# Rows of four tokens for q and k, whole rows for v and out, in a kernel of windowed attention and an MLP

## The chip, the cores and the metric

The kernel runs on one core of a Trainium2 chip. The metric is the device time of one execution in microseconds (us). TensorE is called PE here (PEld is its weight load), VectorE DVE, ScalarE ACT, GpSimd POOL and SyncE SP, as in the profile. Every engine works through its own queue of instructions in order. Transfers (DMAs) are issued by SP and ACT (the hardware queues, q1 and q10 in the profile) and by POOL (the software queue, q0).

## The reference

Attention over a window of 128 tokens and 4 sink tokens, for 4 batches of 8 heads, 768 tokens and 64 values per head, then an MLP with a sigmoid gate over the 3072 rows:

```
scores = q @ k.T / sqrt(64)                       # (4, 8, 768, 768)
keep   = (key < 4) | ((0 <= query - key) & (query - key < 128))
a      = softmax(where(keep, scores, -1e9))
x      = (a @ v), heads side by side              # (3072, 512)
h      = x @ w_in                                 # (3072, 2048)
out    = (h * sigmoid(1.702 h)) @ w_out           # (3072, 512), float32
```

All inputs are float32 in memory. The kernel works in fp16 and sums in float32.

## The kernel before

**Blocks.** The 3072 rows are cut into twelve blocks of 256 tokens (`TB`), three to a batch. For block k the kernel loads q, k and v, casts q and k to fp16, turns them on PE (transposes against `ident`, L447), copies the turned halves out of PSUM into `qkT` (L270), and multiplies keys by queries (L514, and L475 for the sink keys). ACT takes the exponential (L531, L483), DVE multiplies by the mask (L540, L544), PE multiplies by v (L574), DVE divides (L588, L590), PE turns the result (L597) and DVE or ACT copies it to `xT`. The MLP's first product (`mm1`, L631) makes 16 slabs of 128 columns for the block; ACT and DVE form the gate from them (L643, L645). The second product is `mm2`: for block 0 and the last block plainly (L781), for the others with seven products instead of eight of half size (L706), which needs sums of pieces of w_out made once by DVE (`sums`, L659).

**Tokens.** A partition holds two neighbouring tokens of each head, so that a run in memory is 2 x 64 float32 values, 512 bytes. A tile of 128 tokens therefore comes out of the transposes in two groups, the even and the odd tokens; v is loaded in the same order, by four transfers a block of 64 partitions each (L413), and the rows of `out` are written by two transfers of every second row for each 128 tokens (L756, L809). The mask and the places of the sink keys are made for that order. The last block goes back to natural order in its copies to `xT`.

**The plan.** The order of each engine's queue is worked out when the kernel is built. Every operation is given to `Plan` with the engines that may do it, an assumed duration, what it depends on and a due time (`prio`); `Plan.run` walks through time, gives each free engine the ready operation that is due first, and writes the instructions in that order. The chip does not know the plan's times. An instruction waits there only for what its data need (a tile that another engine writes or still reads) and, if it issues a DMA, for the one of eight places of its kind (eight for hardware queues, eight for the software queue) that it takes over from the DMA issued eight before it.

**Loads at the start.** `LOADS` puts the first transfers in order: a0 and v0 (block 0's q and k, and its v), a1, w0 (the first of four pieces of w_in), v1, w1, w2, w3, then the four pieces of w_out as w4, w6, w5, w7, then a2 and v2. q and k of block 0 come in eight transfers by head pairs, from SP and ACT (L369); those of later blocks in one transfer for q and one for k, from SP (L377). v and the weights are issued by POOL (L413, L333). `GATES` makes SP wait, before block 2's q, for w5 to land: SP issues a tiny transfer that reads it (L384). The casts of q and k are DVE's and ACT's for block 0, also POOL's for block 1, and POOL's alone from block 2 on.

**PE's order at the start** is attention of blocks 0 and 1 with `mm1` of block 0, then `mm1` of block 1 mixed with `mm2` of block 0 (64 and 32 matmuls, the latter of 512 columns), and only then the transposes of block 2, the first four matmuls into a bank from `qk16` of that block.

Of the kernel before, what the change touches and what calls it, by code (L numbers as in the profile page):

```python
# [15 lines left out]
D = 64  # L16
# [6 lines left out]
class Op:  # L23
    def __init__(self, engs, fn, deps, prio, acq, rel, kind):

        self.engs, self.fn = engs, fn
        self.deps = [d for d in dict.fromkeys(deps) if d is not None]
        self.prio, self.acq, self.rel, self.kind = prio, acq, rel, kind
        self.eng = self.start = self.end = self.banks = self.places = self.behind = None
        self.users = []  # L30

# [14 lines left out]
class Plan:  # L46
# [14 lines left out]
    def run(self, warm=None, warm_until=0.0, late_bank=0.0):  # L61
# [44 lines left out]
        while todo:  # L106
# [57 lines left out]
            for owner, i in o.rel:  # L164
                t = o.end + 80
                bank_free[owner.banks[i]] = t
                count[owner.acq[0]][owner.places[i]] = t
# [16 lines left out]
def kernel(  # L184
# [27 lines left out]
    SEVEN_FROM = 1  # L212
    NH = NF // 2
# [25 lines left out]
    qkT = ring("qkT", RKT, (P, 2, 2, NP, P), FP16)  # L239
# [17 lines left out]
    def f16(o, i=0):  # L257
        return bank[o.banks[i]][:, 0:256].bitcast(FP16)
# [30 lines left out]
    def make_mask():  # L289


        m = mask.rearrange("s (g u i a) -> s u g i a", g=2, u=2, i=2)
        nc.gpsimd.memset(mask, 1.0)
        for u, (keep, sign) in enumerate(((ALU.is_ge, 1), (ALU.is_gt, -1))):
            for h in range(2):
                a_ = m[64 * h : 64 * h + 64, u]
                nc.gpsimd.affine_select(out=a_, in_=a_, compare_op=keep, fill=0.0, base=-h * sign,
                                        pattern=[[0, 2], [sign, 2], [2 * sign, 64]], channel_multiplier=-2 * sign)
        for h in range(2):
            nc.gpsimd.memset(mask[64 * h : 64 * h + n_sink // 2, 0 : 2 * P], 1.0)  # L300

    o_ident = op("POOL", 350, 450, make_ident, prio=NEVER, kind="const")
    o_mask = op("POOL", 3000, 3100, make_mask, prio=NEVER + 1, kind="const")
# [37 lines left out]
    LOADS = ["a0", "v0", "a1", "w0", "v1", "w1", "w2", "w3", "w4", "w6", "w5", "w7", "a2", "v2"]  # L341

    GATES = {2: 5}
# [13 lines left out]
    def load(k):  # L357
# [4 lines left out]
        war = reuse("s32", sl)  # L362
        dst = qk32[sl].rearrange("p (e h i d) -> p e h i d", e=2, h=H, i=2)
        lq = {}
        if k == 0:
            for p in range(NP):
                for e, (eng, dma, src) in enumerate((("SP", nc.sync, q), ("ACT", nc.scalar, k_ap))):
                    def f(p=p, e=e, dma=dma, src=src):
                        dma.dma_start(  # L369
                            dst[:, e, 2 * p : 2 * p + 2],  # L370
                            src[b, 2 * p : 2 * p + 2, t0 : t0 + TB].rearrange("h (p i) d -> p h i d", i=2),
                        )
                    lq[p, e] = op(eng, 500, (450,), f, war, prio=NEVER + 2.5 + p / 8, kind="load")
        else:
            for e, src in enumerate((q, k_ap)):
                def f(e=e, src=src):
                    nc.sync.dma_start(  # L377
                        dst[:, e], src[b, :, t0 : t0 + TB].rearrange("h (p i) d -> p h i d", i=2)
                    )
                if k in GATES and e == 0:  # L380

                    j = GATES[k]
                    seen = w_in16[0:1, 0, 512 * j : 512 * j + 32] if j < 4 else w_out16[0:1, 4 * (j - 4), 0:32]
                    loads.append(op("SP", 100, (10,), lambda seen=seen: nc.sync.dma_start(gate, seen),  # L384
                                    [(o_win if j < 4 else o_wout)[2 * (j % 4)]], prio=prio - 0.1, kind="gate"))
                o = op("SP", 450, (1800,), f, war, prio=prio + 0.1 * e, kind="load")
                loads.append(o)
                for p in range(NP):
                    lq[p, e] = o

        c16 = qk16[k % RQ].rearrange("p (i e h d) -> p i e h d", i=2, e=2, h=H)
        war = reuse("qk16", k % RQ)
        w = 2 if k == 0 else 4
        for h0 in range(0, H, w):
            for e in range(2):
                def f(eng, h=slice(h0, h0 + w), e=e):
                    copy(eng, c16[:, :, e, h].rearrange("s i h d -> s h i d"), dst[:, e, h])

                ps = range(h0 // 2, (h0 + w) // 2)
                o = plan.any(cast(P * w, CAST_QK[k]), f, [lq[p, e] for p in ps] + war,  # L400
                             prio=nominal(k - 1, -7 + h0) if k else NEVER + h0, kind="cqk")
                for p in ps:
                    o_cqk[k, p, e] = o
        for o in {id(x): x for (kk, _, _), x in o_cqk.items() if kk == k}.values():
            uses("s32", sl, o)
        w16 = v16[k % RV]
        war = reuse("v16", k % RV)

        o_cv[k] = []
        for j in range(2):  # L410
            for i in range(2):
                src = v[b, :, t0 + P * j : t0 + P * j + P].rearrange("h (a i) d -> i a h d", i=2)[i]
                o = op("POOL", ISSUE, (600,), lambda i=i, j=j, src=src: nc.gpsimd.dma_start(  # L413
                    w16[64 * i : 64 * i + 64, j, :, 0:D], src), war + [o_ones],
                       prio=load_at(f"v{k}"), kind="load")
                loads.append(o)
                o_cv[k].append(o)
        if r == 0:

            def f():  # L420
                for t in range(2):
                    for i in range(2):
                        nc.gpsimd.tensor_copy(
                            out=vs16[64 * t + 32 * i : 64 * t + 32 * i + 2, b, :, i],
                            in_=w16[64 * t : 64 * t + 2, 0, i::2, 0:E],
                        )
            o_vs[b] = op("POOL", 1900, 2000, f, [*o_cv[k], o_vs0], prio=nominal(k - 1, 0), kind="vs")
# [4 lines left out]
    o_qkT, o_ks, o_se, o_m, o_xT = {}, {}, {}, {}, {}  # L432

    def front(k, p):
# [6 lines left out]
        c16 = qk16[k % RQ].rearrange("p (i e h d) -> p i e h d", i=2, e=2, h=H)  # L441

        def tp():
            ps = f16(o_tp).rearrange("d (e j i p) -> d e j i p", e=2, j=2, i=2)
            for i in range(2):
                for e in range(2):
                    nc.tensor.transpose(  # L447
                        ps[:, e, :, i, :], c16[:, i, e, 2 * p : 2 * p + 2].rearrange("s h d -> s (h d)"), ident
                    )

        if p == 0:
            o_T["war", k] = reuse("qkT", k % RKT)
        war = o_T["war", k]
        o_tp = op("PE", 4 * pe_ns(P), 3 * pe_ns(P) + P / 2.4 + 166, tp,
                  [o_cqk[k, p, 0], o_cqk[k, p, 1], o_ident] + war, prio=base - 5 * h8, acq=("t", 1), kind="tp")
        uses("qk16", k % RQ, o_tp)
# [426 lines left out]
```

## Time and profile before

| what | value |
|---|---|
| three runs | 230.84, 233.15, 233.51 us; median 233.15 |
| the profiled execution | 232.8 us, of which the core's span is 231.1 |
| busy in the span | PE 220.3 us, DVE 186.5, ACT 138.7, POOL 83.4 |
| mm1, L631 | 768 matmuls of 256 columns, 101.9 us |
| transposes of q and k, L447 | 192 matmuls, 18.8 us |
| copies of them to qkT, L270 | DVE 30 of 415 ns, ACT 18 of 586 ns |
| casts of q and k on POOL, L270 | 40 of 695 ns |
| issues of v on POOL, L413 | 48 of 698 ns |
| q and k of one block from SP | 2 x 512 KB; 7.4 and 8.4 us from issue to landing |
| out | 45 transfers of 128 KB; 2.6 us to landing |
| software queue | 29568 packets, 7.34 MB written, 33.2% of 16 engines' span |
| hardware queue of SP | 27808 packets, 18.22 MB, 30.5% |

A matmul's end is modelled in the profile, so a busy PE need not be at its peak; and sizes of packets are as written, so that a load that is cast from float32 to fp16 on its way counts half of what it reads. The mean granted clock was 0.993.

### The profile page before, as it was taken

How to read it: one execution, taken by the hardware profiler on the slowest of the kernel's cores; microseconds unless marked ns; L12 is line 12 of the kernel's file. 1: busy time of each engine (PE TensorE's matmuls, PEld its weight loads, DVE VectorE, ACT ScalarE, POOL GpSimd, SP SyncE). 2: the span in 40 equal slices, each digit the busy share in tenths (PEclk: the TensorE clock that was granted, in tenths of full speed). 3: DMA queues.
4: the chain of work that ended last, by engine and by line, in shares of the span. 5: the costliest groups of instructions: out<-in, count | busy, mean ns of one | idle time of the engine just before them, and what ended most of it. 6: DMA issues, size and time to landing. Idle time of an engine off the chain costs nothing.

```text
span 231.1 us, 6404 instructions
## 1 busy us (share of the span) xinstructions
PE 220.3 (95%) x2552; PEld 186.5 (81%) x2552; DVE 186.5 (81%) x424; ACT 138.7 (60%) x288; POOL 83.4 (36%) x157
## 2 busy tenths in 40 slices
PE   8869999899999999999999999999999999999994
PEld 7657786588888888988888988888988988898863
DVE  6657979889999979979979969979979869878520
ACT  3717653478688657657567657647657657634320
POOL 8769422399985342275524042233200000000000
PEclk9979999999999999999999999999999999999999
DMA  6999999999999655389215742064012012012042
GB/s 188 239 154 196 187 202 201 263 252 262 158 236 258 112 69 135 97 64 212 92 45 126 131 53 63 1 43 99 3 44 50 0 36 58 3 35 61 0 94 91
DMA packets 58639, 26.64 MB, mean 115 GB/s; under 512 B 26736, under 2 KB 55664, under 8 KB 58608
## 3 DMA queue, kind: packets, MB, share of 16 engines
q0 software_dynamic: 29568, 7.34, 33.2%
q1 hardware_dynamic: 27808, 18.22, 30.5%
q10 hardware_dynamic: 1232, 0.66, 1.0%
q8 instruction: 20, 0.33, 0.6%
q14 instruction: 11, 0.09, 0.1%
HBM read 27.26 MB, written 6.29 MB: 145 GB/s over the span
## 4 chain that ended last, share of the span: by engine, by line
PE 59%; DVE 16%; DMA 13%; POOL 5%; issue 3%; ACT 2%; SPq 0%; POOLq 0%; ACTq 0%; DVEq 0%
PE bank L631 24%; PE bank L706 21%; DMA w_out<-in_moe_w_out_dram 6%; DVE gT L645 4%; DMA v<-in_v_dram 4%; PE bank L574 3%; DMA qk<-in_q_dram 3%; PE bank L781 3%; DVE sm L676 3%; DVE at L540 3%; PE bank L447 3%; PE bank L514 2%; DVE xn L590 2%; PE bank L597 2%; ACT at L531 1%
## 5 line engine op out<-in xcount | busy, mean ns | idle before, releaser
L631 PE MATMUL bank<-xT,w_in 128*128 128x256 f16 x768 | 101.9, 273 | 0.2 <-DVE gT L645 0.2
L643 ACT ACTIVATE th<-bank 128x512 f16<-128x512 f32 x96 | 57.7, 601 | 48.1 <-PE bank L631 40.4
L631 PEld LDWEIGHTS <-w_in 128*128 128x128 f16 x768 | 71.9, 98 | 10.1 <-issue 1.8
L645 DVE SCALAR_TENSOR_TENSOR gT<-th,bank 128x512 f16<-128x512 f16 x96 | 64.9, 681 | 12.3 <-ACT th L643 11.7
L531 ACT ACTIVATE at<-bank 128x512 f16<-128x512 f32 (+1 forms) x96 | 49.4, 573 | 12.6 <-PE bank L514 11.5
L413 POOL DMA_DIRECT2D v<-in_v_dram x48 | 33.0, 698 | 24.7 <-PE bank L574 11.1
L270 POOL CAST qk<-qk 128x512 f16<-128x512 f32 x40 | 26.6, 695 | 33.0 <-PE bank L447 22.6
L706 PE MATMUL bank<-wt,sm 128*128 128x256 f16 x240 | 33.3, 273 | 0.6 <-DVE xT L270 0.6
L706 PEld LDWEIGHTS <-sm 128*128 128x128 f16 x320 | 29.9, 98 | 4.8 <-DVE sm L676 0.7
L540 DVE TENSOR_TENSOR at<-at,mask 128x1024 f16<-128x1024 f16 x32 | 22.5, 712 | 6.4 <-ACT at L531 6.3
L706 PEld LDWEIGHTS <-gT 128*128 128x128 f16 x240 | 22.5, 98 | 2.5
L574 PE MATMUL bank<-v,at 128*128 128x65 f16 x352 | 21.8, 195 | 2.7 <-DMA v<-in_v_dram 2.7
L706 PE MATMUL bank<-w_out,gT 128*128 128x256 f16 x160 | 21.4, 273 | 0.0
L731 DVE SCALAR_TENSOR_TENSOR osb<-bank,osb 128x256 f32<-128x256 f32 x50 | 20.5, 410 | 0.6 <-PE bank L706 0.6
L574 PEld LDWEIGHTS <-at 128*128 128x128 f16 x352 | 17.8, 99 | 3.7 <-DMA v<-in_v_dram 2.9
L590 DVE TENSOR_TENSOR xn<-bank,rcp 128x256 f16<-128x256 f32 x48 | 20.0, 417 | 0.5
L447 PE MATMUL bank<-ident,qk 128*128 128x128 f16 x192 | 18.8, 223 | 1.3 <-POOL qk L270 1.3
L483 ACT ACTIVATE ats<-bank 128x256 f16<-128x256 f32 x32 | 12.8, 401 | 9.0 <-PE bank L475 8.5
L447 PEld LDWEIGHTS <-qk 128*128 128x128 f16 x192 | 13.8, 100 | 2.8 <-POOL qk L270 1.5
L781 PE MATMUL bank<-w_out,gT 128*128 128x512 f16 (+1 forms) x80 | 15.0, 336 | 0.0
L597 PE MATMUL bank<-ident,xn 128*128 128x128 f16 x96 | 13.7, 226 | 1.3 <-DVE xn L590 1.2
L270 DVE COPY qkT<-bank 128x512 f16<-128x512 f16 x30 | 12.4, 415 | 3.2 <-PE bank L447 2.8
(48 smaller groups left out, 246.7 us busy)
## 6 DMA issues: line engine op xcount, KB each, us to landing
out_dram<-osb SPq DMA_DIRECT2D x45, 128.0 KB, 2.6
qk<-in_q_dram SPq DMA_DIRECT2D x11, 512.0 KB, 7.4
qk<-in_k_dram SPq DMA_DIRECT2D x11, 512.0 KB, 8.4
v<-in_v_dram POOLq DMA_DIRECT2D x48, 64.0 KB, 5.6
w_in<-in_moe_w_in_dram POOLq DMA_DIRECT2D x4, 512.0 KB, 8.5
w_out<-in_moe_w_out_dram POOLq DMA_DIRECT2D x4, 512.0 KB, 12.9
qk<-in_q_dram SPq DMA_DIRECT2D x4, 128.0 KB, 3.5
qk<-in_k_dram ACTq DMA_DIRECT2D x4, 128.0 KB, 3.7
```

The costliest lines, as they stand in the source:

```text
L270: {"POOL": nc.gpsimd.tensor_copy, "DVE": nc.vector.tensor_copy, "ACT": nc.scalar.copy}[e](out=out, in_=in_)
L413: o = op("POOL", ISSUE, (600,), lambda i=i, j=j, src=src: nc.gpsimd.dma_start(w16[64 * i : 64 * i + 64, j, :, 0:D], src), war + [o_ones], ...
L447: nc.tensor.transpose(ps[:, e, :, i, :], c16[:, i, e, 2 * p : 2 * p + 2].rearrange("s h d -> s (h d)"), ident)
L531: nc.scalar.activation(out=A[:, i, 0:W], in_=f32(o_s, 2 * n + i)[:, 0:W], func=AF.Exp, scale=scale)
L540: nc.vector.tensor_tensor(out=a_, in0=a_, in1=m_[:, 2 * P :].unsqueeze(1).to_broadcast((P, 4, 2 * P)), op=ALU.mult,)
L574: nc.tensor.matmul(avp()[:, j, i], a_, v_, start=(n == 0), stop=(n == len(mms) - 1))
L590: o_n = op("DVE", 333, 425, lambda: nc.vector.tensor_tensor(out=X[:, p].rearrange("s j (h d) -> s j h d", h=2), in0=avp()[:, :, :, 0:D], i ...
L631: nc.tensor.matmul(f32(holder[0])[:, bass.ts(e, TB)], w_in16[:, c, bass.ts(Fi, P)], X[:, c], start=(c == 0), stop=(c == NP - 1),)
L643: o_t = op("ACT", 477, 600, lambda first=first: nc.scalar.activation(out=th[first.places[0]], in_=f32(first), func=AF.Tanh, scale=0.851), ...
L645: o_g[k, s] = op("DVE", 595, 690, lambda first=first, s=s: nc.vector.scalar_tensor_tensor(out=g[:, 2 * s : 2 * s + 2].rearrange("p a t -> ...
L706: nc.tensor.matmul(f32(holder[bank_of])[:, 0:HM], x[:, Fi], w[:, Fi], start=first and Fi == 0, stop=Fi == NH - 1, skip_group_check=True)
L781: nc.tensor.matmul(f32(holder[0])[:, 0:w], g[:, Fi, bass.ts(j, P)], w_out16[:, Fi, c], start=(n + h == 0), stop=(n + h == NS),)
```

## The change

What it does, piece by piece:

- q and k are loaded with four tokens of a head in a partition (runs of 1 KB). A head's 256 tokens fill 64 partitions, so heads 0 to 3 lie in partitions 0 to 63 and heads 4 to 7 in 64 to 127, and each of q and k takes two transfers of 64 partitions (`g`) a block; for blocks 0 and 1 each is halved again by heads (`m`). A block from 2 on has four transfers of 256 KB where it had two of 512 KB.
- A new function `turn(k, m)` makes eight transposes into one whole bank of PSUM. Two copies take the bank out, one for each head pair, and put the tokens into natural order: they read with a step of 64 elements between neighbours. The bank is free when both are done (`readers = 2`).
- `qkT` is now (query or key, pair, token) in natural order; scores, sink keys, mask, v and out follow. v is two transfers of 128 partitions a block, out one transfer of 128 whole rows for each 128 tokens. Pairs are met in the order `HP = (0, 2, 1, 3)`, which the indices of v and w_in undo.
- Loads at the start: `o_go`, a memset of one element of block 1's q and k tile by POOL, is put after v0's issues, and SP's loads of block 1 wait for it; w0 is put after the sink keys of block 0's first two pairs; in `LOADS` a2 and v2 come before w_out; block 2's q and k wait for w2 and block 3's for w5.

The diff, cut to its core:

```diff
-    LOADS = ["a0", "v0", "a1", "w0", "v1", "w1", "w2", "w3", "w4", "w6", "w5", "w7", "a2", "v2"]
-    GATES = {2: 5}
+    LOADS = ["a0", "v0", "a1", "w0", "v1", "w1", "w2", "w3", "a2", "v2", "w4", "w6", "w5", "w7"]
+    GATES = {2: 2, 3: 5}
...
+    o_go = op("POOL", 80, 180, lambda: nc.gpsimd.memset(qk32[1][0:1, 0:1], 0.0), prio=NEVER + 14, kind="const")
...
-        war = reuse("s32", sl)
-        dst = qk32[sl].rearrange("p (e h i d) -> p e h i d", e=2, h=H, i=2)
+        war = reuse("s32", sl) + ([o_go] if k == 1 else [])
+        dst = qk32[sl].rearrange("p (e m x f) -> p e m x f", e=2, m=2, x=2)
...
+        n = 2 if k <= 1 else 1
+        for c in range(n):
+            ms = slice(c * 2 // n, (c + 1) * 2 // n)
+            for e, src in enumerate((q, k_ap)):
+                eng = "ACT" if (k, e) == (0, 1) else "SP"
+                for g in range(2):
+                    h0 = 4 * g + 2 * ms.start
+                    to = dst[64 * g : 64 * g + 64, e, ms].rearrange("p m x f -> p (m x) f")
+                    fr = src[b, h0 : h0 + 4 // n, t0 : t0 + TB].rearrange("h (a i) d -> a h (i d)", i=4)
+                    o = op(eng, 500, (730 / n,), lambda to=to, fr=fr, eng=eng: (
+                        nc.scalar if eng == "ACT" else nc.sync).dma_start(to, fr), war,
+                           prio=prio + 0.1 * (4 * c + 2 * e + g), kind="load")
...
-            for i in range(2):
-                src = v[b, :, t0 + P * j : t0 + P * j + P].rearrange("h (a i) d -> i a h d", i=2)[i]
-                o = op("POOL", ISSUE, (600,), lambda i=i, j=j, src=src: nc.gpsimd.dma_start(
-                    w16[64 * i : 64 * i + 64, j, :, 0:D], src), war + [o_ones],
+            src = v[b, :, t0 + P * j : t0 + P * j + P].rearrange("h s d -> s h d")
+            o = op("POOL", ISSUE, (1250,), lambda j=j, src=src: nc.gpsimd.dma_start(w16[:, j, :, 0:D], src),
...
+    def turn(k, m):
+        c16 = qk16[k % RQ].rearrange("p (m i e f) -> p m i e f", m=2, i=4, e=2)[:, m]
+        def tp():
+            ps = f16(o_tp).rearrange("d (g e i a) -> d e i g a", g=2, e=2, i=4)
+            for e in range(2):
+                for i in range(4):
+                    nc.tensor.transpose(ps[:, e, i], c16[:, i, e], ident)
...
+        o_tp.readers = 2
+        for g in range(2):
+            p = 2 * m + g
+            def cp(e, g=g, p=p):
+                copy(e, T[:, :, p].rearrange("d e (a i) -> d e a i", i=4),
+                     f16(o_tp)[:, 512 * g : 512 * g + 512].rearrange("d (e i a) -> d e a i", e=2, i=4))
+            o_qkT[k, p] = [plan.any(pick({"DVE": (600, 690), "ACT": (477, 600)}, COPY[k]), cp, [o_tp] + war,
+                                    prio=base + 2 * g * h8 - 5 * h8, rel=[(o_tp, 0)], kind="cp")]
...
-            for i in range(2):
-                def f(to=paired[i], fr=T[j][64 * i : 64 * i + 64], i=i):
-                    nc.sync.dma_start(to, fr)
-                o_d = op("SP", 500, (400.0,), f, after, prio=prio, kind="out")
+            o_d = op("SP", 500, (800.0,), lambda to=rows, fr=T[j]: nc.sync.dma_start(to, fr), after, prio=prio, kind="out")
...
+        for m_ in range(2):
+            turn(k_, m_)
...
+        if k_ == 0:
+            o_w[0].deps.append(o_ks[0, 1])
```

What the build makes of it, engine by engine: PE has the same matmuls apart from four more of its idle fillers. Of the 48 copies to `qkT` DVE does 22 and ACT 26 (before 30 and 18). The tile framework lets one engine at a time read a bank: in 18 of the 22 DVE copies the wait is for ACT's copy of the bank's other half, in the rest ACT waits for DVE or one engine does both. POOL issues 24 transfers of v, and after w3 its queue reads v2, w4, w6, w5, then the four casts of block 2, then w7 and v3; w4, w6 and w5 wait there only for the places that w0 and v1 held. PE's queue has, after attention of blocks 0 and 1, the 64 matmuls of `mm1` of block 0 and 24 of block 1's, and then the transposes of block 2; the other 40 of block 1's `mm1` and all of `mm2` of block 0 stand behind these.

## The prediction, made before the changed kernel was run

> **What bounds the kernel now.** I read the page first: PE is busy for 95% of the span, so time is won or lost where PE's order stops. The second view is the chain that ended last, in order of time, for the first 50 us (start, duration, what):
>
> ```profile
> 19.07 0.68 POOL w_in L333
> 19.75 1.45 POOL w_out L333 x2
> 21.20 13.77 DMA w_out<-in_moe_w_out_dram
> 34.99 0.63 SPq L384
> 35.66 7.13 DMA qk<-in_q_dram
> ...
> 45.54 0.87 POOL qk L270
> 46.45 0.56 PE bank L447 x7
> ```
>
> Block 2's q is issued at 35.66, when w5 has landed. It needs 7.13 us, k lands about 45.5, POOL casts it, and PE goes on with block 2's transposes at 46.45. Before that PE had run nearly without a hole from 27 us on and had finished `mm1` of blocks 0 and 1 and `mm2` of block 0. I call the 46.45 T, the time at which block 2's transposes can go on.
>
> Why did q take 7.13 us? The third view is the DMA queues, for the window from 35.7 to 38.0 us and then for 38 to 42 (queue: packets, MB, share of 16 engines):
>
> ```profile
> q0 software_dynamic: 2391, 0.33, 213.0%
> q1 hardware_dynamic: 40, 0.01, 2.5%
> ```
> ```profile
> q1 hardware_dynamic: 1892, 0.95, 92.1%
> q0 software_dynamic: 829, 0.10, 40.5%
> ```
>
> The hardware queue, though it had been given q, got almost nothing until about 38.0, when the software queue had finished what it was given earlier: w7, v2 and three of the four pieces of v3. The opposite case is from 6 to 9 us, where v0 had been issued from 4.50 on, but block 1's q and k at 3.50 and 3.92:
>
> ```profile
> q1 hardware_dynamic: 1739, 0.88, 109.2%
> ```
>
> No packet of v moved in that window. So both queues together are served about in the order of issue. This is the reading that my number hangs on.
>
> In the later blocks DVE is nearly full too. One block, in a window of 17 us (length, then busy PE, PEld, DVE, ACT, POOL):
>
> ```profile
> 94.00:111.00 17.00, 17.00 (x202) 14.86 (x200) 14.55 (x34) 11.52 (x25) 10.13 (x21) 1.00 0.83 122
> ```
>
> Over such windows from 77 to 213 us DVE is busy 14.3 to 15.2 of 17 us.
>
> **PE's order around block 2.** In the chain 48 matmuls of L781, 16384 columns, take 6.96 us, 0.109 us for 256 columns. The changed order leaves 40 matmuls of block 1's `mm1` (4.4 us) and `mm2` of block 0 (16384 columns, 7.0 us) behind block 2's transposes: 11.3 us of work that was ahead of them. If nothing else changed, the kernel would end at the same time for T = 46.45 - 11.3 = 35.1 us. Each microsecond of T above that is lost, and below it won, as far as PE arrives that early itself.
>
> **When PE arrives.** It needs w3 first. In the trace the weights land at about 2.54 us each (POOL's issues of v, let go by them, start at 27.63, 30.17, 32.71 and 35.26). w3 landed at about 27.5. The same bytes must come before w3 now; two things shorten it. The hole from 15 to 16 us (68 GB/s written there, 201 from 29 to 35) goes, 0.7 us: it came when POOL waited 2.77 us for a place held by v0, and with two issues of v a block that wait is gone. And 1-KB rows: the trace has no load with them; 512-byte rows moved at 294 GB/s (6 to 9 us), the weights' 2-KB rows at 1.05 MB in 2.54 us, 413 GB/s. I take 340, nearer to the 512-byte row, so that q and k of two blocks, 2.1 MB, take 6.2 us instead of 7.1: 0.9 us won (0 to 2.0). So w3 lands at 25.9, 16 matmuls end `mm1` of block 0 at 27.7, 24 more end at 30.3. v0 landed at 12.7; now it is issued 1.4 us earlier (three instructions of the mask fewer, 2 x 0.42 and 0.35, with hops) and without the 3 us of block 1's packets ahead of it. That moves attention of block 0 by some 4 us, but PE then waits for the weights, so the gain is contained in the 30.3.
>
> **When block 2 arrives.** SP now issues a2 when w2 has landed, 24.8 - 1.6 = 23.2 us. But POOL has by then issued v2, w4, w6 and w5: they wait only for places that w0 and v1 give back, and v1's last piece, issued at 12.97, had landed 4.8 us later, at 17.8, even before. By the order of issue a2 stands behind them. In the old run the software queue was through at 38.0; now w7 (2.54 us) and three quarters of v3 are no longer ahead (v moved 0.33 MB written, 0.66 read, in 2.3 us, so 0.39 MB takes 1.4), and 0.7 and 0.9 are saved as above: 38.0 - 2.5 - 1.4 - 0.7 - 0.9 = 32.5. From there to the landing of k it was 7.5 us with block 3's q behind it; at the least it is the transfer at the weights' rate, 2.5, plus 0.6. Block 3 now comes later, so I take 5.0, between the two. Then the cast and PE's start, 0.95 as before (45.5 to 46.45): T = 38.45. Bounds: 31.4 + 3.1 + 0.95 = 35.4 and 33.4 + 7.5 + 0.95 = 41.9. PE stands from 30.3 to 38.4, where it stood 1.5 us before. That is 3.35 us over break-even (0.3 to 6.8).
>
> The 11.3 us of matmuls now run beside more DVE work: the sums of w_out, 16 of 0.417 us, were done in the old stall's cover and stand now behind block 2's transposes. I take the pace of the later blocks for them: these come 17.28 us apart (an exponential on the chain starts at 84.70 and, two blocks on, at 119.26), and their matmuls at 0.109 us make 16.3. That is 6% of 11.3, 0.7 us (0 to 2).
>
> w7 is behind the casts of block 2 in POOL's queue: issued at about 41.5, landed at about 47. PE asks for it some 8 us of work after T, at 46.5. I take 0, at most 1.
>
> **The copies.** The last block of the old kernel already copies with a step of 64 elements into `xT`. DVE's copies in 201 to 207 us (stepped) and 160 to 196 (mostly plain; min/median/max):
>
> ```profile
> L270 DVE COPY xT<-bank x2: 424/424/424, 200.7 to 204.6; 128x256 f16<-128x256 f16 x2
> ```
> ```profile
> L270 DVE COPY xT<-bank x5: 277/291/292, 162.8 to 187.4; 128x256 f16<-128x256 f16 x5
> ```
>
> 133 ns more for 256 elements, so 266 for 512: 415 becomes 680. DVE: 22 x 0.68 - 30 x 0.415 = +2.5 us in all, 0.2 a block. ACT showed 367 ns for either kind: +8 x 0.586 = 4.7 us on an engine that is 60% busy, nothing on the path. The new thing is the wait of the second copy for the first: 18 times DVE stands for up to 0.6 us, with the mask multiplications, divisions and gates of other blocks queued behind it; ACT's gates and PE's products with v wait for those. Per block that is up to 1.2 + 0.2 of the 1.8 to 2.7 us that DVE has left. PE itself has at least 2.9 us of matmuls between a pair's transposes and their first reader from block 3 on, so the copies are not late. Bounds 0 and 18 x 0.6 = 10.8; I take 1.5, near the low end, for the spare time covers the mean.
>
> The Trainium skill speaks against two copies of one bank at once: PSUM — Partial Sum Buffer, "PSUM bank collisions raise a hardware error", says that two engines must not be on one bank and quadrant together, reads against reads included. By that page the waits must stay; without them the 1.5 would be 0. No run here shows two engines reading one bank at once.
>
> **Edits that cost nothing.** 24 fewer issues of v at 0.698 us (each of the 24 left has twice the rows: 0.7 to 1.4 us) free 0 to 16.7 us of POOL, which is busy 36%; from block 3 on its casts are early. out in whole rows: 24 transfers from SP instead of 46, behind which only loads stand that are two blocks early; the last block's are unchanged. Sink keys and mask: the same POOL work or less. SP issues 78 transfers instead of 73, 0.4 to 0.6 us each when nothing holds them; behind the wait for w2 in its queue are only the loads of blocks 2 to 4, and block 3's, issued after w5 at about 35, land near 41, where PE asks for them after 50.
>
> **Sum.** 231.1 + 3.35 + 0.7 + 1.5 = 236.65 of span; the profiled execution had 1.7 us around the span: 238.35, so 238. That is 2.1% over the median, 233.15; the profiled execution was 0.15% below it. Bounds of this case: 233 (0.3 and nothing else) to 244 (6.8, 0.7 and 3.5). A run of this kernel can be told from no change at about 2%, from 228.5 to 237.8.
>
> **Rivals.**
> *The queues share.* If the two queues took turns, a2 would run from 24.5 at half the rate (1.05 MB at 180 GB/s, 5.8 us) it would land 1 us later and T would be 32.3: -2.8 + 0.7 + 1.5 = -0.6, 232.2. Against it: the 2.5% above. The Trainium skill, DMA: Bandwidth & Descriptors, "Queues, rings and completion order", has each DMA engine going round the queues packet by packet, which would be this case; the windows above disagree. Chance 0.13.
> *Faster.* The head was bound by bytes before w3. If rows of 1 KB run at the weights' 413 GB/s (2.0 us), v's whole transfers too (1.2 us) and the hole goes (0.7), w3 lands at 23.6, and if a2 then isn't held by w_out, T is PE's own 28: -7.1 + 0.7, 226.4. It decides below T = 30. For it: DMA is the fullest resource until 40 us. Against it: v's packets are still 128 bytes as written. 0.12.
> *DVE becomes the bound.* If half of the 10.8 us of waits reach PE: 231.1 + 3.35 + 0.7 + 5.4 + 1.7 = 242.3. For it: 14.3 to 15.2 of 17 us. Against it: its spare time. 0.17.
> *The enforced order isn't enforced on the chip* is my forecast itself: the order of a2 before w_out is the plan's, and no wait makes POOL keep it.
>
> **Chances.** Forecast 0.58: the bounds put 0.41 of it above 237.8, 0.17 within. Sharing: 0.12 within, 0.01 faster. Faster: 0.12. DVE: 0.16 slower, 0.01 within. Together faster 0.13, same 0.30, slower 0.57. Range 230 to 243.5: it leaves out the faster case and 0.06 at the upper end; the likeliest case alone has 233 to 244.
>
> **What would show it.** PE's first transposes of block 2 (new line L441) at 38 us with a hole of about 8 us before them, released by POOL's casts; the hardware queue near nothing in the DMA view from 24 to 32 us; w3's first matmuls at 26; DVE copies to `qkT` at 0.68 us; DVE at 15 to 16.5 of 17 us per block. I am wrong if q and k of block 2 land by 32 us, or if w_out is issued only after them.

## The result, and the profile after

| | runs | median us | ratio to before, 95% interval |
|---|---|---|---|
| before | 4 | 232.80 | |
| changed | 4 | 242.22 | 1.0414 [1.0344, 1.0484] |

The changed kernel is 9.4 us slower. The predicted 238 us was on the right side of it and 4.2 us short, inside the range of 230 to 243.5. The profiled execution took 242.16 us, with a span of 240.4 (before 231.1) and a mean granted clock of 0.971 (before 0.993).

Three views answer to those of before. First the chain that ended last, from 12.9 us to the transposes of block 2 (start, duration, what):

```profile
12.92 11.49 DMA w_in<-in_moe_w_in_dram
24.43 0.59 SPq L375
...
27.06 12.31 DMA qk<-in_k_dram
...
39.49 0.62 POOL qk L277
...
40.17 0.61 PE bank L441 x4
40.77 0.85 PE bank L627 x4
```

w2 lands at 24.4 us and SP's gate lets block 2's loads go. The last of them, k's upper half, takes 12.31 us from its issue to landing, POOL casts it, and T, the time at which block 2's transposes can go on, is 40.17 us. It was 46.45 before, but 11.3 us of matmuls that were ahead of it now stand behind it.

Second, what TensorE did in the meantime (stretch and its length, then busy PE, PEld, DVE, ACT, POOL, then the granted TensorE clock, the DMA share and GB/s):

```profile
30.00:35.00 5.00, 2.21 (x21) 1.73 (x18) 2.13 (x4) 2.02 (x4) 0.62 (x2) 1.00 1.17 247
35.00:40.00 5.00, 0.40 (x4) 0.23 (x4) 0.00 (x0) 0.00 (x0) 1.05 (x2) 0.53 0.68 141
40.00:45.00 5.00, 4.83 (x36) 3.50 (x37) 2.88 (x5) 2.74 (x6) 3.12 (x5) 0.50 0.67 113
45.00:50.00 5.00, 4.80 (x57) 3.01 (x55) 3.47 (x10) 4.11 (x10) 0.61 (x1) 0.94 1.28 220
```

PE is busy for 2.6 us of the ten from 30 to 40; it runs dry at 32.2. Before, it was busy throughout the same stretch:

```profile
30.00:45.00 15.00, 15.00 (x109) 10.37 (x106) 12.50 (x28) 6.80 (x12) 3.87 (x6) 1.00 1.46 218
```

The column after POOL is what the prediction left out: the clock falls to half in the hole and stays there until about 45.6 us. That is why four matmuls of L627 take 0.85 us in the chain above, where four of 256 columns take 0.44 at full clock.

Third, the DMA queues from 29 to 38 us (packets, MB written, share of 16 engines' time):

```profile
q0 software_dynamic: 1074, 1.06, 69.8%
q1 hardware_dynamic: 1075, 1.04, 42.2%
```

Before that, from 24 to 29 us, the hardware queue moved next to nothing, though SP had issued block 2's q at 25.06:

```profile
q1 hardware_dynamic: 32, 0.00, 0.9%
```

So its first data came some 4 us after the issue (at 29.05). From 29 us on the two queues go packet for packet, 1075 against 1074. A packet of w_out writes 1 KB but reads 2, and holds an engine longer: 69.8% of the engines' time for w4, w6 and w5, 42.2% for block 2. (The shares add to over 100% since packets overlap.)

The copies out of the transposes (busy us, mean ns of one, then idle time before them and what ended it):

```profile
L277 ACT COPY qkT<-bank 128x512 f16<-128x512 f16 x26 | 15.4, 600 | 17.4 <-DVE qkT L277 9.6 <-PE bank L441 6.9 <-issue 0.8
L277 DVE COPY qkT<-bank 128x512 f16<-128x512 f16 x22 | 15.2, 691 | 18.8 <-PE bank L441 10.7 <-ACT qkT L277 7.9
```

DVE's take 691 ns, ACT's 600, and each engine waits for the other's copy of the same bank: ACT 9.6 us in all, of which 8.7 are one wait through the hole, and DVE 7.9 in 14 waits.

Below, the *lag* of TensorE at a time is that time less the useful columns of the matmuls that it has started so far, at 2,400 columns a microsecond, from the trace. Matmuls with zeros are left out, and those over 64 of the 128 rows (keys by queries) count half. The lag grows by what is lost and, in much the same way in all kernels, by these halves. At 30, 50 and 70 us it was 17.3, 19.4 and 21.6 before and is 16.1, 27.7 and 29.3 now: the loss comes between 30 and 50.

### The profile page after: what moved, and what is told of

Read it like the earlier page. It is cut to its first block, busy times and chain, and to the rows that moved or that the text cites. A ratio compares the mean times of both kernels' runs of the same rounds, so it can differ in the third digit from the quotient of the medians.

```text
span 240.4 us, 6388 instructions
## 1 busy us (share of the span) xinstructions
PE 224.1 (93%) x2556; PEld 186.6 (78%) x2556; DVE 183.0 (76%) x413; ACT 141.5 (59%) x295; POOL 64.2 (27%) x123
## 4 chain that ended last, share of the span: by engine, by line
PE 76%; DMA 12%; DVE 6%; POOL 2%; SPq 1%; issue 1%; ACT 1%; ACTq 1%; DVEq 0%; POOLq 0%
PE bank L627 30%; PE bank L702 25%; DMA qk<-in_k_dram 7%; PE bank L575 5%; DMA w_in<-in_moe_w_in_dram 5%; PE bank L515 4%; PE bank L772 4%; PE bank L441 4%; PE bank L598 2%; DVE at L541 1%; PE bank L479 1%; DVE wt L655 1%; ACTq L388 1%; DVE qkT L277 1%; SPq L388 1%
## 5 line engine op out<-in xcount | busy, mean ns | idle before, releaser
L627 PE MATMUL bank<-xT,w_in 128*128 128x256 f16 x768 | 102.7, 275 | 0.0
L627 PEld LDWEIGHTS <-w_in 128*128 128x128 f16 x768 | 72.8, 99 | 11.9 <-issue 3.1
L277 POOL CAST qk<-qk 128x512 f16<-128x512 f32 x40 | 25.4, 662 | 43.5 <-PE bank L441 17.1
L702 PE MATMUL bank<-wt,sm 128*128 128x256 f16 x240 | 34.2, 273 | 0.0
L277 DVE COPY qkT<-bank 128x512 f16<-128x512 f16 x22 | 15.2, 691 | 18.8 <-PE bank L441 10.7
L413 POOL DMA_DIRECT2D v<-in_v_dram x24 | 21.2, 889 | 21.0 <-PE bank L575 20.9
L277 ACT COPY qkT<-bank 128x512 f16<-128x512 f16 x26 | 15.4, 600 | 17.4 <-DVE qkT L277 9.6
L441 PE MATMUL bank<-ident,qk 128*128 128x128 f16 x192 | 15.9, 229 | 9.5 <-POOL qk L277 7.6
L702 PE MATMUL bank<-w_out,gT 128*128 128x256 f16 x160 | 22.7, 272 | 0.0
L575 PEld LDWEIGHTS <-at 128*128 128x128 f16 x352 | 17.3, 97 | 4.5 <-DVE at L541 3.1
L473 POOL COPY ks<-qkT 64x4 f16<-64x4 f16 x32 | 6.7, 210 | 38.1 <-ACT qkT L277 36.0
L575 PE MATMUL bank<-vs,ats 128*128 128x65 f16 x128 | 16.2, 193 | 0.0
```

The source lines that it names most:

```text
L277: {"POOL": nc.gpsimd.tensor_copy, "DVE": nc.vector.tensor_copy, "ACT": nc.scalar.copy}[e](out=out, in_=in_)
L413: o = op("POOL", ISSUE, (1250,), lambda j=j, src=src: nc.gpsimd.dma_start(w16[:, j, :, 0:D], src), war + [o_ones], prio=load_at(f"v{k}"), ...
L441: nc.tensor.transpose(ps[:, e, i], c16[:, i, e], ident)
L575: nc.tensor.matmul(avp()[:, j, i], a_, v_, start=(n == 0), stop=(n == len(mms) - 1))
L627: nc.tensor.matmul(f32(holder[0])[:, bass.ts(e, TB)], w_in16[:, HP[c], bass.ts(Fi, P)], X[:, c], start=(c == 0), stop=(c == NP - 1),)
L702: nc.tensor.matmul(f32(holder[bank_of])[:, 0:HM], x[:, Fi], w[:, Fi], start=first and Fi == 0, stop=Fi == NH - 1, skip_group_check=True)
```

## The experiments

The two sides of the change were parted first, then the loads, then the clock, the order of TensorE's work and the copies. In the table, T is the start of the matmuls of block 2's first bank that wait for k, "PE" its busy time in the 15 us from 30 to 45; both are from the one profiled execution of each kernel.

| kernel | T | PE | us | ratio to before |
|---|---|---|---|---|
| before | 46.45 | 15.0 | 232.80 | |
| changed | 40.17 | 7.4 | 242.22 | 1.0414 [1.0344, 1.0484] |
| new rows, old order of loads | 45.50 | 13.4 | 235.89 | 1.0154 [1.0119, 1.0188] |
| old rows, new order of loads | 41.64 | 7.7 | 241.06 | 1.0380 [1.0343, 1.0417] |
| changed, zeros in the hole | 39.33 | 13.1, zeros among it | 240.55 | 1.0363 [1.0324, 1.0401] |
| changed, w_out behind block 2 | 34.27 | 12.1 | 241.02 | 1.0384 [1.0355, 1.0413] |
| the same, block 3 not gated | 34.56 | 8.6 | 241.48 | 1.0399 [1.0360, 1.0438] |
| new rows, old order, gate at w6 | 44.86 | 14.6 | 237.63 | 1.0205 [1.0147, 1.0263] |
| old rows, old order, gate at w6 | 44.26 | 14.8 | 232.43 | 1.0009 [0.9976, 1.0042] |
| changed, work ahead of block 2 | 40.23 | 14.6 | 233.75 | 1.0052 [1.0027, 1.0078] |
| the same, one engine a bank | 40.38 | 14.2 | 231.45 | 0.9952 [0.9926, 0.9978] |
| the same, halves crossed | 39.81 | 13.6 | 231.17 | 0.9963 [0.9936, 0.9990] |
| new rows, old order, one engine a bank | 46.03 | 13.9 | 233.95 | 1.0083 [1.0048, 1.0118] |
| new rows, old order, halves crossed | 44.63 | 14.4 | 233.09, one run | |

### The order of the loads undone

```diff
-    LOADS = [..., "w3", "a2", "v2", "w4", "w6", "w5", "w7"]
-    GATES = {2: 2, 3: 5}
+    LOADS = [..., "w3", "w4", "w6", "w5", "w7", "a2", "v2"]
+    GATES = {2: 5}
-        war = reuse("s32", sl) + ([o_go] if k == 1 else [])
+        war = reuse("s32", sl)
-            o_w[0].deps.append(o_ks[0, 1])
```

> The changed kernel with the list of loads and the gate of before (the four w_out pieces ahead of block 2, one gate after w3) and without the two added orders (the wait of w0 for block 0, the marker before block 1). Rows of 1 KB, the copies to natural order, v in two transfers and whole out rows stay. Theory (the loss is in the order of the loads: block 2 put behind a gate and shared with w_out): block 2 comes as late as before, but 40 products of the first projection are queued ahead of it again, so there is no hole: T about 46, TensorE clock 0.9 or more in every slice from 10 us on, 231.5 to 235.5 us. Rival (the loss is in the new rows and copies): 238 us or more, with the lag of TensorE behind its useful work growing faster than 0.066 us per us over the later blocks.

235.89 us, between the two: the order of the loads, with the two added waits and the order of work that the plan makes of it, carries 6.3 of the 9.4 us, and the rows and copies the other 3.1 (3.6 by the ratio), a little more than the theory allowed them. There is no long hole. The chain at block 2:

```profile
35.42 6.39 DMA qk<-in_q_dram
...
44.81 0.64 POOL qk L277
...
45.50 0.40 PE bank L440 x4
```

But the lag, 15.0 us at 40 against 17.4 before, is 22.9 at 70 against 21.6. TensorE got to block 2 earlier than before, at 43.4, and then stood for 2.1 us; the clock also fell to half behind this short stand, from 46.9 to about 50. The expectation of 0.9 or more in every slice was wrong there (mean 0.84 from 40 to 50).

### The order of the loads alone

```diff
-    LOADS = [..., "w3", "w4", "w6", "w5", "w7", "a2", "v2"]      # the kernel before
-    GATES = {2: 5}
+    LOADS = [..., "w3", "a2", "v2", "w4", "w6", "w5", "w7"]
+    GATES = {2: 2, 3: 5}
```

> The kernel before with the list of loads and the two gates of the changed kernel; rows of 512 B, order of tokens, v, copies and out rows as before. Theory (the order of the loads is the loss): block 2 shares the 16 engines with w4, w6, w5 packet by packet, and a 512-B packet gets still less than a 1-KB one beside 2-KB reads; T 39 to 45, a hole of 6 to 12 us ahead of it, a clock near 0.5 for some 5 us behind it, 237 to 245 us. Rival (rows and copies are the loss): no hole to speak of beyond that of before, 231 to 235 us.

As the theory had it: T 41.64, PE busy for 0.23 us from 35 to 40, the clock at 0.50 from 40 to 45, 241.06 us. From issue to landing, block 2's k took 16.21 us, with 512-byte packets between those of w_out:

```profile
24.70 16.21 DMA qk<-in_k_dram
...
41.64 0.93 PE bank L447 x7
```

The 8.3 us (241.06 less 232.80) come with no edit of rows, copies, v or out at all. With the 3.1 of the run before they make more than 9.4, so the two don't simply add: here block 2 comes 1.5 us later than with the new rows.

### The clock in the hole

```diff
+            if (k, m) == (2, 0):
+                for _ in range(120):
+                    nc.tensor.matmul(f32(o_tp)[:, 0:P], zero, zero, start=True, stop=True)
             ps = f16(o_tp).rearrange("d (g e i a) -> d e i g a", g=2, e=2, i=4)
```

> The changed kernel with 120 products of zeros (128 columns each, into the bank that block 2's first transposes then overwrite) queued on TensorE directly ahead of those transposes: work is added, none left out. At 128 columns and full clock they take some 7 us, about the hole. Theory (the clock that falls to 0.5 after the hole costs 2.6 to 3 us over and above the stand): T stays at about 40 (39.5 to 41), the clock from 40 to 45 us is 0.9 or more, the time 238.5 to 240.5 us, that is 2 to 3.5 us under the changed kernel. Rival (the clock is only a mark of the stand and costs nothing of its own, as the work behind it waits for something else): within 1 us of the changed kernel's 242.2 us.

The clock is at 1.00 through hole and work:

```profile
35.00:40.00 5.00, 3.86 (x67) 3.64 (x63) 0.24 (x1) 0.00 (x0) 1.34 (x3) 1.00 0.62 122
40.00:45.00 5.00, 4.26 (x53) 2.85 (x50) 4.02 (x7) 4.51 (x11) 2.29 (x3) 1.00 0.70 125
```

The time falls by 1.7 us to 240.55 (the spans of the two profiled executions by 2.3). T was 0.8 us earlier in this execution, so the clock's own price is put between 0.8 and 1.7 us, less than the 2.6 to 3 that was expected. It is near the spread of the runs (239.9 to 241.8 us here, 241.4 to 242.6 for the changed kernel), and the two intervals of the ratio overlap. The stand itself costs more than its clock, as the run on TensorE's order shows.

### Block 2 without w_out beside it

```diff
+        if k_ == 2:
+            for j_ in range(4, 8):
+                o_w[j_].deps.extend(x for (kk, _, _), x in o_cqk.items() if kk == 2)
```

> The changed kernel, with one more order: the four w_out pieces (w4 to w7) are issued by GpSimd only after block 2's q and k have been cast, so block 2 shares the engines with v alone. Theory (sharing with w4, w6, w5 is what makes block 2 late): block 2's q lands by 30 and k by 32 us, T 31 to 34, the hole before it 3 us or less, the clock 0.8 or more behind it; w_out lands 6 to 9 us later than now, by 48 to 54 us, and 229 to 234 us if the second projection of block 0 can wait for it behind block 2's work. Rival 1 (the gate itself, with its start of some 4 us after w2, is what makes it late): T 37 or later and 238 us or more. Rival 2 (w_out becomes the thing that is late): T 31 to 34, but a new stand for w5 or w7 between 45 and 60 us, 235 to 240 us.

T is 34.27, so w_out is what made block 2 late; rival 1 falls. The start is part of it: q's first data came 1.4 us after its issue here (24.91 to 26.34), not 4.0. But only 1.2 us come back. The chain tells where the rest went:

```profile
33.59 0.62 POOL qk L277
...
34.27 0.42 PE bank L441 x4
...
47.71 7.28 DMA qk<-in_q_dram
...
58.48 0.63 POOL qk L277
```

Block 3 waits, by the second gate, for w5, which now lands at 46.4 us; its q is issued at 47.7 and its last cast ends at 59.1. The lag is 21.8 us at 50 (5.9 less than in the changed kernel) and 27.4 at 70 (1.9 less). The stand moved on by a block. Rival 2 was right about that, except that it is block 3 that is waited for, not w_out, and that the time is above its 235 to 240. T alone, then, does not set the time: this one lies under the 35.1 us of the break-even.

### And without the second gate

```diff
-    GATES = {2: 2, 3: 5}
+    GATES = {2: 2}
```

> The changed kernel with w_out issued behind block 2's casts, as in the run of that name (241.0 us), and without the second gate: block 3's q and k are issued right behind block 2's and no longer wait for w5, which landed at 46.4 us there. Theory (in that run the stand only moved from block 2 to block 3, whose transposes went on at 59.2 us): T stays at 34 to 35, block 3's q and k land by 42 us, the lag of TensorE at 70 us is 23.5 to 25 us in place of 27.4, the time 236.5 to 238.5 us. Rival (w_out, later by the 1 MB of block 3, is then waited for): the lag at 70 us is 26.5 us or more, 239.5 us or more.

241.48 us, the rival. With block 3's loads ahead of w_out as well, w4 is what comes late, and TensorE stands 2.6 us for it:

```profile
35.01 9.40 DMA w_out<-in_moe_w_out_dram
44.46 2.74 PE bank L772 x6
```

So in three orders of the loads something is late between 34 and 59 us, whichever is put last: block 2, block 3 or w_out. Either all of TensorE's work that could be done was waiting behind the late thing in its queue, or there was none. The run on TensorE's order tells which for the changed kernel.

### Block 2 earlier in the old order

```diff
-    GATES = {2: 5}
+    GATES = {2: 6}
```

> The kernel with the new rows and the old order of loads (235.9 us), with one number changed: block 2's q and k wait for the third w_out piece (w6, landed at 31.5 us there) and not for the last but one (w5, 34.1). Theory (what is left of its loss to before is that block 2 still comes late: TensorE stood 2.1 us ahead of its transposes at 45.5, though it was 2.4 us ahead of before at 40): block 2 lands 2.6 us earlier, T 42.5 to 44, 232.5 to 234.5 us. Rival (the rest of the loss is in the copies and their waits from 45 us on): T earlier as well, but the lag at 70 us and the time stay within 1 us of that kernel, 235 to 236.5 us.

> The kernel before with the one number changed: block 2's q and k wait for w6 in place of w5. Theory (before, TensorE stood 1.3 us ahead of block 2's transposes at 46.45, and block 2 lands some 2.5 us earlier now): T 44.5 to 45.5, that is as soon as TensorE gets there, and 230.8 to 232 us, 0.2 to 1.3 us under before. Rival (packets of block 2 now share with w7 and gain nothing, or push w7 back): 232 us or more.

Neither gained. With the new rows block 2's k landed at 44.05 us in place of 44.16, though issued 1.4 us earlier, as w7 and v2 were still in flight; T went from 45.50 to 44.86 only, where 42.5 to 44 was expected, and the time did not fall (237.63; its runs spread from 235.6 to 239.5, so no more is read from it). With the old rows T went from 46.45 to 44.26 and TensorE stood 0.25 us, yet the time is that of before, 1.0009 [0.9976, 1.0042]. So the stand of before was worth less than these runs can tell.

### TensorE's order, with the changed kernel's own loads

The planner takes all loads to be served in the order of issue. Here it is told that block 2's come 7 us later than that:

```diff
-                o.end = dma_free + (500 if lat[0] < 500 else 1100)
-                landed[e == "POOL"].append(o.end)
+                landed[e == "POOL"].append(dma_free + (500 if lat[0] < 500 else 1100))
+                o.end = landed[e == "POOL"][-1] + getattr(o, "late", 0)
...
+                    if k == 2:
+                        o.late = 7000
```

> The changed kernel (242.2 us) with its own loads in its own order, but with the planner told that block 2's q and k come 7 us later than it works out. What the planner then writes down differs in TensorE's order above all: all 128 products of the first projection (88 before) and 12 of the second stand ahead of block 2's transposes; w7 is issued with the other w_out pieces and not behind block 2's casts. Theory (the loss in the order part is the stand: the planner puts block 2's transposes ahead of work that could be done, and they come later than it thinks): block 2's first transposes at 39 to 41.5 as now, TensorE stands 2 us or less between 30 and 42 in place of some 7, the clock 0.9 or more behind it, the lag at 50 us 20 to 23 in place of 27.7, 234.5 to 237.5 us. Rival (the head is bound by what the loads bring, in any order of TensorE's work): the stand moves to w_out or v, lag at 60 us 26 or more, 239 us or more.

233.75 us, 8.5 us under the changed kernel and better than expected. T is 40.23 (of the eight transposes below the last four wait for k): block 2 comes as late as it did, but TensorE has work up to that moment (start, duration; L629 is the first projection, L774 the second, L443 the transposes):

```profile
35.81 1.47 PE L629 MATMUL bank<-xT,w_in 128*128 128x256 f16 x12
37.12 2.75 PE L774 MATMUL bank<-w_out,gT 128*128 128x512 f16 x12
39.71 0.91 PE L443 MATMUL bank<-ident,qk 128*128 128x128 f16 x8
```

PE is busy for 14.6 of the 15 us from 30 to 45, the clock stays at 1.00, and the lag at 50 us is 18.9, below that of before (19.4). This settles the main cause: what cost 8.5 us is the order of work that the planner made of landing times that were too early, with block 2's transposes queued ahead of work that was ready. Not all of it need be the stand of TensorE, for the plan moved more than that: DVE's sums of w_out ran from 49.6 to 57.7 us in the changed kernel and run from 39.3 to 49.5 here, and w7 is issued at 21.95 and not at 40.61. In the changed kernel no engine waited for w7; what the sums' place is worth was not tried alone. The loads' new order costs nothing that can be seen here: the kernel is 2.1 us better than the one with the old order and the same rows (233.75 against 235.89; by their ratios to before, 1.0052 against 1.0154). That doesn't make the new order the better one, since the plan of the old order was not mended in this way and TensorE stood 2.1 us in it.

### Both copies of a bank on one engine

```diff
-            o_qkT[k, p] = [plan.any(pick({...}, COPY[k]), cp, [o_tp] + war,
+            o_qkT[k, p] = [plan.any(pick({...}, ("DVE", "ACT")[(k + m) % 2]), cp, [o_tp] + war,
```

> The kernel with the new rows and the old order of loads (235.9 us), with both copies out of a bank of transposes on one engine (VectorE and ScalarE by turns, bank by bank), where now one goes to each. No work is added or left out. Theory (a copy that waits in VectorE's queue for the copy of the other engine holds the work behind it; the idle time of VectorE ahead of its copies put down to ScalarE's copy is 10.3 us over the run): that idle time falls under 3 us, the time by 1 to 2.5 us, to 233.4 to 235. Rival (that idle time is off the path, as TensorE has other work queued): 235 to 236.8 us, no change that can be told.

> The kernel of the run before with both copies out of a bank on one engine, as in the run on the old order, where that was worth 1.9 us. Theory (the two losses are separate and add): 232.5 to 235.5 us, 1 to 2.5 us under the run before. Rival (the copies' waits were covered or worth less here): within 1 us of the run before.

On the old order of loads it is worth 1.9 us (235.89 to 233.95), on the kernel of the section before 2.3 (233.75 to 231.45). Both theories hold (the second time lies under its range, as the kernel that it was made from came out better than expected), and the second kernel is half a per cent under the one before the change: 0.9952 [0.9926, 0.9978]. The group of DVE's copies in the kernel of the section before and then in this one:

```profile
L277 DVE COPY qkT<-bank 128x512 f16<-128x512 f16 x23 | 15.8, 689 | 10.7 <-ACT qkT L277 8.6 <-PE bank L443 1.9
L277 DVE COPY qkT<-bank 128x512 f16<-128x512 f16 x24 | 15.9, 682 | 0.9 <-PE bank L443 0.8
```

The copies are as long as they were, 682 ns against 689; the idle time ahead of them falls from 10.7 to 0.9 us, and none of it is put down to ACT any more. Most of the gain is in the later blocks: from 70 to 220 us the lag grows by 7.9 us (21.8 to 29.7), with a bank's copies on two engines by 9.8 (22.3 to 32.1).

### The halves of the partitions

```diff
-                for g in range(2):
+                for g in ((1, 0) if eng == "ACT" else (0, 1)):
```

> The kernel with the new rows and the old order of loads (235.9 us), with ScalarE issuing block 0's k upper half first, so that the two queues write opposite halves of the partitions at a time. Theory (the new rows come slower than the old ones, 228 to 260 GB/s from 4 to 6 us where before moved 294, since both queues' transfers of 64 partitions write the same half): block 0's last landing falls from 8.1 to 7.5 us or less and the packets' median from 73 ns; the time may stay within 1 us. Rival (it is the packets of 1 KB or v0's small packets beside them, not the half): block 0's last landing 7.9 us or later.

> The best kernel so far (work ahead of block 2, both copies of a bank on one engine: 231.45 us, ratio to before 0.9952) with block 0's halves crossed as well. It settles the single look at the crossed halves, whose time came out 2.8 us under the kernel it was made from although block 0 landed no earlier (8.94 us against 8.14). If the crossing is worth something by itself: 228.5 to 230.5 us, ratio 0.990 or less. Rival (that difference was one between executions and chips: in that run's profile 256-KB transfers of block 2 landed 0.87 us apart, in the other's 1.17): 230.8 to 232.3 us, ratio 0.993 to 0.998.

Block 0's last landing was 8.94 us, later than the 8.09 without the edit: the theory of the halves falls. The single time of 233.09 us, 2.8 under the kernel that it was made from, has no counterpart on the other kernel, 231.17 against 231.45, which can't be told apart. What differed in that one execution were the transfers of blocks 2 and 3, on which it has no edit. The stretch from 40 to 45 us in the kernel without the edit and then with it (the last number is GB/s):

```profile
40.00:45.00 5.00, 3.42 (x27) 2.35 (x25) 2.87 (x5) 1.94 (x4) 3.03 (x5) 1.00 1.13 224
```
```profile
40.00:45.00 5.00, 4.36 (x37) 3.03 (x36) 3.30 (x7) 2.18 (x4) 4.62 (x6) 1.00 1.09 318
```

The same instructions moved 224 GB/s in one execution and 318 in the other. Why is open; it was not tried. The two ran on different chips, and block 2's four transfers landed 1.17 us apart in the one and 0.88 in the other.

## Why the prediction was right

The first step of the prediction held for this kernel: T comes after the break-even of 35.1 us, and 11.3 us of ready work now stand behind block 2's transposes. A plan that gives TensorE such work ahead of T, with block 2 landing as late as it did, brought 8.5 us. The side was right for this reason, and so was that w_out would make block 2 late, though w_out goes beside it and not ahead of it. Term by term:

- **T over break-even**, 3.35 us forecast (T = 38.45), 5.07 measured (40.17). The term was mis-sized, and the step under it, "both queues together are served about in the order of issue", was wrong. The profile shows two things instead: some 4 us from SP's issue to the first packet of data, and then packet for packet with the software queue. The 4 us go with w_out too: over all 14 kernels, block 2's first data came 3.6 to 4.3 us after the issue in the eight in which two or more pieces of w_out had been issued and were still to land, and 1.4 to 2.0 in the six with one piece or none. What holds it back isn't shown. The Trainium skill, DMA: Bandwidth & Descriptors, "Queues, rings and completion order", has each engine going round the queues that have work, a packet from each; from 29 to 38 us the trace agrees (1075 packets against 1074), and the windows of before that the forecast relied on can be read so too: what was issued later had not begun. That T came out within 1.7 us is partly luck: by either reading w4, w6 and most of w5 pass before block 2's last packets.
- **When PE arrives**, forecast 30.3, measured 32.2. The forecast has TensorE stand for w3, and it did not: its last 40 matmuls before the hole ran from 27.68 without a gap, behind other work. The arrival does not enter the sum, as T is later. w3 landed at 26.9 where 25.9 was forecast. Rows of 1 KB were taken at 340 GB/s. Block 1's, all but alone on the engines from 10.6 to 12.3 us, moved at 256, less than the 294 of the old rows. So that gain was no gain.
- **The clock** was no term at all. It cost 0.8 to 1.7 us by the run with zeros, and with T makes most of what is missing in the sum.
- **The copies**: 1.5 us forecast, 1.9 and 2.3 measured. Mechanism and place were right (DVE's queue held by the other engine's copy), and so was the duration, 0.68 us. The wait between the two copies could be removed without two engines on one bank.
- **The pace** of the displaced matmuls, 0.7 us, and w7 at 0 us: w7 landed at 47.8 and does not appear in the chain; the pace was not measured by itself.

With the measured terms, and the 0.7 as it was forecast: 231.1 + 5.07 + 1.3 (about the middle for the clock) + 2.1 (the middle for the copies) + 0.7 = 240.3 of span, where the profile has 240.4. So close a sum is no test of its terms. By the runs the plan's order cost 8.5 us, more than T, the clock and the pace make together (7.1), and the copies 2.3; without the two losses the new rows and loads are 1.1 us better than before by the ratio (0.9952), which the sum does not have. What makes up the difference was not measured.

Of the rivals, *the queues share* had the mechanism of the later part, packet for packet, and the wrong price. It started block 2's data at 24.5 us and gave it half of the rate, T = 32.3; they started at 29.0, with one packet of 1 KB to each that reads 2. The time of *DVE becomes the bound*, 242.3, is the measured one by chance: the waits of the copies reach TensorE with 2 us, not 5.4. *Faster* needed w3 at 23.6 us and a2 not held by w_out; neither came. Of the signs named, TensorE's hole, POOL's casts as its releaser, DVE's copies at 0.68 us and DVE at 15 of 17 us (15.07 from 94 to 111) came true; the hardware queue was quiet up to 29 us only, not 32, and w3's first matmuls came at 27.7, not 26.

## What to carry to other kernels

A planned order is only as good as the landing times that the plan assumes: where a load shares the engines with another queue, put ready work ahead of its first reader, and give the plan the landing that the trace shows. A stand of TensorE is priced by the work that is stuck behind it in its queue, and where it lasts for microseconds add the lower clock that follows. When two engines each take half of one bank, try one engine for both halves: here that was worth 1.9 and 2.3 us, more than the loss that was left.

## What the runs showed of the hardware

**A short stand can cost the clock too.** The Trainium skill, TensorE: Matmul & The Clock Gate, "What's actually happening", has the clock halved after an idle window of about 3.4 us and back after as long a busy one. The long hole agrees for the fall: TensorE ran dry at 32.2 us and the clock fell at 35.3, 3.1 us later. It came back at 45.6, 5.4 us after work had begun again. But with the new rows and the old order it stood only 2.1 us, from 43.4 to 45.5, and the clock still went to half at 46.9, 1.4 us after work had begun again, for some 3.4 us. In the same kernel with the copies on one engine, a stand of the same length, 43.9 to 46.0, left the clock alone in the profiled execution. That is one execution of each: the mean clock of the latter's other six, 0.978 to 0.990 against 0.997, shows more time at half speed in each of them, without saying where. What decides isn't shown. The stretch from 47 to 48 us in the one and in the other:

```profile
47.00:48.00 1.00, 1.00 (x13) 0.64 (x13) 0.84 (x2) 0.73 (x3) 1.00 (x2) 0.50 1.12 270
```
```profile
47.00:48.00 1.00, 1.00 (x15) 0.94 (x14) 1.00 (x3) 0.60 (x2) 0.86 (x2) 1.00 1.11 298
```

**Longer rows were not faster.** Rows of 1 KB in transfers of 64 partitions moved at 256 GB/s where rows of 512 bytes in transfers of 128 partitions had moved at 294, and between two executions the stretch with the same transfers ranged from 224 to 318 GB/s. Neither the row nor the half of the partitions was shown to be the cause.
